# Turning the gated rows for token mixing: TensorE transposes replaced by VectorE block transposes and a DRAM round trip

## The chip, the cores and the metric

The kernel runs on one core of one Trainium2 chip. The metric is the device time of one execution in microseconds; the time before is the median of three runs. All times below are microseconds unless they are marked ns.

## What is computed

Attention with sigmoid weights over 4 batches of 12 heads (448 rows, head size 64), then a gated feed-forward block on x of 4 x 448 x 768, then a token and channel mixer:

```python
xk = mu_k * x + (1 - mu_k) * x_prev        # x_prev: x one row earlier
xr = mu_r * x + (1 - mu_r) * x_prev
k  = np.maximum(xk @ w_k, 0.0)             # 768 -> 1024
v  = k * k @ w_v                           # 1024 -> 768
y  = sigmoid(xr @ w_r) * v                 # the gated rows
h  = np.maximum(y.transpose(0, 2, 1) @ w_tok1, 0.0) @ w_tok2   # 448 -> 256 -> 448
u  = y + h.transpose(0, 2, 1)
out = u + np.maximum(u @ w_ch1, 0.0) @ w_ch2                   # 768 -> 1536 -> 768
```

The kernel keeps channels on partitions and tokens in the free dimension. Only the token mixing contracts over tokens, so y has to be turned once before it.

## The kernel before, in words

The four batches are worked on in two halves of two batches (`for b0 in range(0, B, 2)`, L526): `attention`, `first_part`, `second_part`. Each of the 768 channels is in one of NT = 6 tiles of 128; a tile holds 896 tokens of two batches (W = 2 S). Every product of this kernel is made of three float32r passes: operands are split into a high and a low part, and high times high, high times low and low times high are summed (`products`, L336). `products` runs a first column piece of 512 and one of 384 over all inner tiles, and after each second inner tile it calls `tick()`, which emits one pending step of the weight pipeline.

The weight pipeline (L264 to L310) is in program order on each engine. A weight w is loaded by SP into one of two `raw` buffers (`w_raw`), formed by two ScalarE instructions (`w_form`, L236 and L237), joined by two VectorE instructions (`w_join`, L240 and L243; the end of a join frees the raw buffer and lets SP issue the load of the weight after next), its high part is written by ScalarE (`w_high`, L281) and its low part by VectorE (`w_low`, L285). Weights of `w_v` and `w_tok1` are 128x512, all others here are 128x768.

`first_part` first makes r (L421), then k (L430), then six rows of `w_v` products (L441). "Row m" below is the m-th of these six: TensorE multiplies with two weights (part 0 and part 1), and at its end VectorE multiplies the result into `rows[:, m]` (L448). These are the gated rows. In row m, in the second column piece of part 0, `y_transpose(m - 1)` (L362) turns the row before: eight TensorE transposes against an identity (L368) into a PSUM tile, then ScalarE and VectorE write the high and the low part (L370, L371), and for the last 64 tokens a high part on partitions 0 to 63 and a low part on 64 to 127 (L372, L373). The last row, `y_transpose(5)`, is turned inside the first piece of the first token product.

The token mixing is six small products of w_tok1 and six of w_tok2. In this text tok1(p) is the p-th piece of L455 (p = 0 to 2, each makes h1 of two channel tiles m = 2p and 2p + 1; ScalarE L467, VectorE L468 write its two parts), and tok2(m) the product of L474 that adds h of tile m to `rows[:, m]` (L480). Before, all three tok1 come first and then all six tok2. `u`, the input of the channel mixing, is split into two parts by ScalarE (L481) and VectorE (L472), after each tok2. `u`, `y` and the inputs of k lie in the same memory `two`, so that `u` can't be written before the last use of `y`. The first product of `second_part` ("f = 0" below) runs its two column pieces in turn, tile by tile, so that it needs u of tile 5 last.

The order of instructions of each engine is the order of the program (`manual_schedule`, L67): no scheduler moves them, and an engine that waits holds all that is behind it.

Of the kernel before, what the change touches and what calls it, by code (L numbers as in the profile page):

```python
# [8 lines left out]

F32 = mybir.dt.float32  # L10
F32R = mybir.dt.float32r
# [11 lines left out]
P = 128  # L23
# [3 lines left out]
W = 2 * S  # L27

WIDE = ((0, 512), (512, W - 512))
WARM = 26  # L30
HALF = 3 * P + S

# [6 lines left out]
def kernel(  # L39
# [23 lines left out]
    wraw, wpool, wsplit = pool("wraw", 2), pool("wpool", 2), pool("wsplit", 3)  # L63
    tmps = pool("tmps", 2)
    psum = pool("psum", 4, space=PSUM)

    ctx.enter_context(tc.manual_schedule())  # L67

# [4 lines left out]


    warm = const.tile([P, 1], F32, tag="warm", name="warm")
    ident = const.tile([P, P], F32, tag="ident", name="ident")
    mus = {n: [const.tile([P, NT], F32, tag=m + n, name=m + n) for m in ("mu", "om")] for n in "kr"}
    xes = [const.tile([P, 2, 1 + S], F32, tag="xe%d" % i, name="xe") for i in range(NT)]
    const.tile([P, 8], F32, tag="pad", name="pad")
# [33 lines left out]
    def new_ps():  # L113
        return psum.tile([P, 1024], F32, tag="ps", name="ps")
# [29 lines left out]
    load_v(0)  # L144
    load_v(1)

    make_identity(nc, ident)

    for t in xes:
        POOL.memset(t[:, :, 0:1], 0.0)  # L150

    att = {}

# [205 lines left out]
    def against(w, x, kt):  # L359
        return [(w[0][:, t], w[1][:, t], x[0][:, t], x[1][:, t]) for t in range(kt)]  # L360

    def y_transpose(m):  # L362
        ps = new_ps()
        psv = ps.rearrange("p (r b c) -> p r b c", r=4, b=2)
        for r in range(4):
            n = P if r < 3 else TAIL
            for b in range(2):
                PE.transpose(psv[:n, r, b], rows[:, m, b * S + r * P : b * S + r * P + n], ident)  # L368
        hi, lo = (t[:, :, m] for t in y)
        ACT.copy(hi[:, :3], psv[:, :3])  # L370
        DVE.tensor_tensor(out=lo[:, :3], in0=psv[:, :3], in1=f32(hi[:, :3]), op=ALU.subtract)  # L371
        ACT.copy(hi[:TAIL, 3], psv[:TAIL, 3])  # L372
        DVE.tensor_tensor(out=hi[TAIL:, 3], in0=psv[:TAIL, 3], in1=f32(hi[:TAIL, 3]), op=ALU.subtract)  # L373

    def attention(b0):
        end = (b0 + 2) * NPAIR

        def load_more(i):
            if i + 3 < end:
                load_kq(i + 3)  # L380
                load_v(i + 2)
                load_v(i + 3)
            if i + 4 < end:
                load_kq(i + 4)

        for t in range(NT):
            i, xe = b0 * NPAIR + 2 * t, xes[t]
            if t == 0:
                load_kq(i + 2)
            else:  # L390
                load_more(i)
            scores(i)
            if i == 0:
                score_tails(i)
            scores(i + 1)
            if t == 0:
                if i:
                    score_tails(i)
                load_more(i)
                if i == 0:  # L400
                    w_raw(2)
            if t + 1 < NT:
                split_kq(i + 2)
                split_kq(i + 3)
            if b0 == 0 and 1 <= t < 5:
                w_form(t)
                w_join(t)
                w_raw(t + 2)
                w_high(min(t - 1, 3))
                w_low(min(t - 1, 3))  # L410
            ps = [values(i), values(i + 1)]
            if t + 1 < NT:
                score_tails(i + 2)
            value_tails(i, ps[0], xe)
            value_tails(i + 1, ps[1], xe)
            mix("r", t, xr, xe)

    def first_part(b0):
        if b0 == 0:
            tok2_load()  # L420
        for m in range(NT):  # L421
            w = weights()
            ps = new_ps()
            products(ps, WIDE, against(w, xr, NT), in_turn=m == 0)
            ACT.activation(rows[:, m], ps[:, :W], AF.Sigmoid)
            mix("k", m, xk, xes[m])
            if b0 == 0 and m < 3:
                tok2_stage(m)

        for m in range(F // P):  # L430
            w = weights()
            ps = new_ps()
            products(ps, WIDE, against(w, xk, NT))
            hi, lo = kk(m)
            t = tmps.tile([P, W], F32, tag="tmp", name="sq")
            ACT.activation(t, ps[:, :W], AF.Relu)
            DVE.tensor_tensor(out=t, in0=t, in1=t, op=ALU.mult)
            ACT.copy(hi, t)
            DVE.tensor_tensor(out=lo, in0=t, in1=f32(hi), op=ALU.subtract)

        for m in range(NT):  # L441
            ps = new_ps()
            for part in range(2):
                w = weights()
                parts = [(w[0][:, t], w[1][:, t], *kk(4 * part + t)) for t in range(4)]
                hooks = {0: lambda: y_transpose(m - 1)} if m and part == 0 else {}
                products(ps, WIDE, parts, 4 * part, 8, hooks)
            DVE.tensor_tensor(out=rows[:, m], in0=rows[:, m], in1=ps[:, :W], op=ALU.mult)  # L448

        wt1 = [weights()]  # L450
        i = use[0]
        use[0] += 1
        wt1.append(halves.pop(i))
        due.extend([lambda: w_form(i + 4), lambda: None, lambda: w_join(i + 4), lambda: w_raw(i + 6)])
        for piece in range(3):  # L455
            ps = new_ps()
            ms = slice(2 * piece, 2 * piece + 2)
            for j in range(2):
                wh, wl = wt1[j]
                x = [t[:, :, ms].rearrange("p r m b c -> p r (m b c)") for t in y]  # L460
                parts = [(wh[:, r], wl[:, r], x[0][:, r], x[1][:, r] if r < 3 else None) for r in range(4)]
                products(ps[:, j * 512 : (j + 1) * 512], ((0, 512),), parts)
                if piece == 0 and j == 1:
                    y_transpose(NT - 1)
# [4 lines left out]
        due.extend([lambda: w_high(i + 3), lambda: w_low(i + 3)])  # L469
# [4 lines left out]
        for m in range(NT):  # L474
# [6 lines left out]
            ACT.copy(u[0][:, m], rows[:, m])  # L481
            if m:
                u_low(m - 1)
        u_low(NT - 1)

    def second_part(b0):
        for half in range(2):
# [44 lines left out]
def lay_out(x):  # L532

    import numpy as np

    def chunks(w, parts=1):

        kt = w.shape[0] // (P * parts)
        w = w.reshape(parts, kt, P, w.shape[1] // P, P).transpose(3, 0, 2, 1, 4)
        return w.reshape(-1, P, kt * P)  # L540

    qt = x["q"].transpose(0, 1, 3, 2).reshape(B * NPAIR, P, S)
    kt = x["k"].transpose(0, 1, 3, 2).reshape(B * NPAIR, P, S)
# [4 lines left out]
    y = {  # L548
        "q": qt,
        "k": np.concatenate([kt[:, :, 3 * P :], kt[:, :, : 3 * P]], axis=2),  # L550
        "v": np.concatenate([head, tail], axis=2),
        "moe_mu_k": x["moe_mu_k"].reshape(NT, P).T,
        "moe_mu_r": x["moe_mu_r"].reshape(NT, P).T,
        "moe_w_k": chunks(x["moe_w_k"]),
        "moe_w_v": chunks(x["moe_w_v"], 2),
        "moe_w_r": chunks(x["moe_w_r"]),
        "moe2_w_tok1": chunks(np.concatenate([x["moe2_w_tok1"], x["moe2_w_tok1"][3 * P :]])),
        "moe2_w_tok2": x["moe2_w_tok2"],
        "moe2_w_ch1": chunks(x["moe2_w_ch1"]),
        "moe2_w_ch2": chunks(x["moe2_w_ch2"], 2),  # L560
    }
# [44 lines left out]
```

## Time and profile before

| | |
|---|---|
| time, median of 3 runs | 869.82 us (869.79 to 870.35) |
| the profiled execution's own time | 870.03 us |
| its span | 868.2 us |
| PE busy | 863.7 us (99%) |
| PEld (weight loads, beside PE) | 728.8 us (84%) |
| DVE busy | 539.3 us (62%) |
| ACT busy | 407.1 us (47%) |
| POOL busy | 1.0 us |
| moved by DMA | 98.12 MB |

PE is TensorE, DVE is VectorE, ACT is ScalarE, POOL is GpSimd and SP the engine that issues most DMAs. The profiled execution took 0.21 us more than the median. The busy share says how much of the span an engine had an instruction; where a time of the engine is not on the chain that ends last, it costs nothing.

### The profile page before, as it was taken

To read this page: it belongs to the slowest core of one execution; us is meant where nothing else is said; L and a number is where in the kernel's file an instruction comes from. 1 tells how busy PE (TensorE), PEld (TensorE's weight loads), DVE (VectorE), ACT (ScalarE), POOL (GpSimd) and SP (SyncE) were. 2 spreads that over 40 slices of the span, in tenths; PEclk is the share of its full clock that TensorE was granted. 3 is DMA by queue.
4 is the path that set the end of the run, shared out by engine and by line. 5 is a ranking of instruction groups with operands and counts; after the bars stand their busy time and mean duration, and the time that the engine had idled before them with its cause. 6 is when DMAs were issued, how large, how long until landed. Compare 5 with 4: busy or idle time off the path is not lost.

```text
span 868.2 us, 11307 instructions
## 1 busy us (share of the span) xinstructions
PE 863.7 (99%) x4616; PEld 728.8 (84%) x4616; DVE 539.3 (62%) x610; ACT 407.1 (47%) x538; POOL 1.0 (0%) x13
## 2 busy tenths in 40 slices
PE   9999999999999999999999999999999999999998
PEld 5558989899888989898955598989998998989897
DVE  4877966556676555555656598666566755554551
ACT  6884455444544433443356644455445444334420
POOL 0000000000000000000000000000000000000000
PEclk9999999999999999999999999999999999999999
DMA  8532332233412333334664133222334033333321
GB/s 279 194 129 79 109 109 85 74 98 97 140 67 75 110 123 102 103 108 164 223 206 132 40 109 109 88 94 74 97 98 165 18 109 109 109 109 110 109 100 63
DMA packets 29571, 98.12 MB, mean 113 GB/s; under 512 B 3536, under 2 KB 15952, under 8 KB 29520
## 3 DMA queue, kind: packets, MB, share of 16 engines
q1 hardware_dynamic: 29232, 96.95, 33.6%
q8 instruction: 36, 0.59, 0.3%
q10 hardware_dynamic: 288, 0.46, 0.1%
q14 instruction: 15, 0.12, 0.1%
HBM read 91.89 MB, written 5.51 MB: 112 GB/s over the span
## 4 chain that ended last, share of the span: by engine, by line
PE 99%; DVE 0%; issue 0%; POOL 0%; POOLq 0%
PE ps L347 84%; PE ps L209 6%; PE ps L182 6%; PE ps L198 1%; PE ps L368 1%; PE ps L217 1%; PE ps L141 0%; DVE rows L506 0%; POOL rows L138 0%; POOLq L592 0%
## 5 line engine op out<-in xcount | busy, mean ns | idle before, releaser
L347 PE MATMUL ps<-one,whi 128*128 128x512 f32 (+1 forms) x1152 | 323.6, 363 | 0.0
L347 PE MATMUL ps<-two,whi 128*128 128x512 f32 (+1 forms) x1044 | 295.8, 365 | 0.0
L347 PEld LDWEIGHTS ps<-one,whi 128*128 128x128 f32 x1152 | 211.5, 188 | 24.8 <-issue 1.4
L347 PEld LDWEIGHTS ps<-two,whi 128*128 128x128 f32 x1044 | 192.5, 188 | 23.1 <-DVE two L371 0.4
L347 PE MATMUL ps<-one,wlo 128*128 128x512 f32 (+1 forms) x576 | 207.3, 363 | 0.0
L347 PE MATMUL ps<-two,wlo 128*128 128x512 f32 (+1 forms) x528 | 191.1, 366 | 0.0
L281 ACT CAST whi<-wd 128x768 fp32r<-128x768 f32 (+1 forms) x104 | 80.7, 776 | 134.6 <-PE ps L347 93.6
L347 PEld LDWEIGHTS ps<-one,wlo 128*128 128x128 f32 x576 | 107.9, 188 | 11.3
L240 DVE SCALAR_TENSOR_TENSOR wd<-wd,raw 128x768 uint32<-128x768 uint32 (+1 forms) x104 | 92.2, 886 | 32.8 <-ACT raw L237 32.5
L347 PEld LDWEIGHTS ps<-two,wlo 128*128 128x128 f32 x528 | 99.0, 188 | 11.4
L285 DVE TENSOR_TENSOR wlo<-wd,whi 128x768 fp32r<-128x768 f32 (+1 forms) x104 | 91.6, 880 | 9.4 <-ACT whi L281 8.9
L243 DVE SCALAR_TENSOR_TENSOR wd<-raw,wd 128x768 uint32<-128x768 uint32 (+1 forms) x104 | 92.2, 886 | 3.6
L236 ACT ACTIVATE wd<-raw 128x768 f32<-128x768 f32 (+1 forms) x104 | 88.4, 850 | 3.9 <-DMA raw<-in_moe_w_ch_dram 2.3
L237 ACT ACTIVATE raw<-raw 128x768 uint32<-128x768 uint32 (+1 forms) x104 | 86.9, 836 | 0.0
L494 DVE SCALAR_TENSOR_TENSOR one<-ps,one 128x896 fp32r<-128x896 f32 x24 | 26.2, 1092 | 71.0 <-ACT one L493 71.0
L512 DVE TENSOR_TENSOR rows<-rows,ps 128x896 f32<-128x896 f32 x23 | 25.0, 1087 | 67.8 <-PE ps L347 67.8
L493 ACT ACTIVATE one<-ps 128x896 fp32r<-128x896 f32 x24 | 22.1, 921 | 95.8 <-PE ps L347 95.8
L190 ACT ACTIVATE rows<-ps 128x896 f32<-128x896 f32 x72 | 60.2, 967 | 9.4 <-PE ps L182 8.9
L209 PE MATMUL ps<-rows,vn 128*64 128x448 f32 x288 | 56.8, 543 | 0.0
L182 PEld LDWEIGHTS ps<-two 64*128 64x128 f32 x414 | 37.9, 184 | 10.9 <-PE ps L198 6.3
L209 PEld LDWEIGHTS ps<-rows,vn 128*64 128x64 f32 x288 | 19.6, 137 | 31.9 <-issue 27.6
L182 PE MATMUL ps<-two 64*128 64x448 f32 x414 | 45.2, 368 | 0.0
(67 smaller groups left out, 533.8 us busy)
## 6 DMA issues: line engine op xcount, KB each, us to landing
raw<-in_moe_w_ch_dram SPq DMA_DIRECT2D x48, 768.0 KB, 4.1
raw<-in_moe_w_k_dram SPq DMA_DIRECT2D x16, 768.0 KB, 4.2
raw<-in_moe_w_v_dram SPq DMA_DIRECT2D x24, 512.0 KB, 3.6
raw<-in_moe_w_r_dram SPq DMA_DIRECT2D x12, 768.0 KB, 4.3
vn<-in_v_dram SPq DMA_DIRECT2D x24, 224.0 KB, 4.3
kq<-in_k_dram SPq DMA_DIRECT2D x23, 224.0 KB, 4.2
kq<-in_q_dram SPq DMA_DIRECT2D x23, 224.0 KB, 4.3
out_dram<-rows SPq DMA_DIRECT2D x23, 224.0 KB, 2.1
```

The source lines that it names most:

```text
L182: PE.matmul(ps[:, h * 512 : h * 512 + S], x[me, c * P : (c + 1) * P], y[me], start=(n == 0), stop=(n == len(passes) - 1),)
L190: ACT.activation(a, banks(ps), AF.Sigmoid, bias=-math.log(S), scale=1.0 / math.sqrt(D))
L209: PE.matmul(ps[h * D : h * D + D, :S], vns[i % 4][:, 3 * h + c], att[i % 2, c][:, h], start=(c == 0), stop=False)
L236: ACT.activation(f32(dst), f32(raw[..., 1]), AF.Copy, scale=2.0**-112)
L237: ACT.activation(raw[..., 0], raw[..., 0], AF.Copy, bias=0.4375, scale=0.875 * 2.0**-29)
L240: DVE.scalar_tensor_tensor(out=dst, in0=dst, scalar=3, in1=raw[..., 0], op0=ALU.logical_shift_left, op1=ALU.bitwise_or)
L243: DVE.scalar_tensor_tensor(out=dst, in0=raw[..., 1], scalar=0x80000000, in1=dst, op0=ALU.bitwise_and, op1=ALU.bitwise_or)
L281: ACT.copy(halves[i][0], forms[i])
L285: DVE.tensor_tensor(out=halves[i][1], in0=forms.pop(i), in1=f32(halves[i][0]), op=ALU.subtract)
L347: PE.matmul(ps[:, a : a + cols], w, x[:, a : a + cols], start=(i == 0 and n == 0), stop=(i == count - 1 and n == len(passes) - 1),)
L494: DVE.scalar_tensor_tensor(out=lo, in0=ps[:, :W], scalar=0.0, in1=f32(hi), op0=ALU.max, op1=ALU.subtract)
L512: DVE.tensor_tensor(out=rows[:, m], in0=rows[:, m], in1=ps[:, :W], op=ALU.add)
```

## The change

The TensorE transposes, their PSUM tile and the identity are gone. In their place, for each row m:

- `y_turn(m)`: three VectorE STREAM_TRANSPOSE instructions turn 32x32 blocks of `rows[:, m]` into a buffer `turned` (768 columns of both batches, then the last 64 tokens twice with 128 columns each).
- `y_out(m)`: a DMA that ScalarE issues writes the buffer (512 KB) to a DRAM tile `blocks`.
- `y_in(m)`: a DMA that ScalarE issues reads it back into `staged` in another order, so that the blocks of one token group stand beside each other: 4 pieces of 1 KB for each of 128 partitions. It waits for `y_out(m)`.
- `y_split(m)`: ScalarE writes the high part (L405) and VectorE the low part (L406). For the last 64 tokens, which stand on the partitions twice, ScalarE multiplies with `sign` (L407), VectorE multiplies the staged copy with `latter` (L409) and adds (L410), so that half of the partitions get the high part and half the low part.

`turned` and `staged` (two buffers each) lie in the memory of `xes`, whose first column is therefore zeroed by POOL again in each `attention`. The rows of w_tok1 are permuted on the host to the order that the blocks have. `latter` and `sign` are made once, by POOL and VectorE, at the start.

The token mixing is written in another order: tok1(0), tok1(1), tok2(0), tok2(1), tok2(2), tok1(2), tok2(3), tok2(4), tok2(5), with the split of row 4 behind tok1(0), the split of row 5 behind tok2(1), and all splits of u behind tok1(2).

```diff
-    def y_transpose(m):
...
+    def y_turn(m):
+        src = beside(rows[:, m])
+        dst = turned[m % 2].rearrange("p d r b c -> p b r d c")
+        DVE.transpose(dst[:, :, :3], src[:, :, : 3 * P].rearrange("p b (r d c) -> p b r d c", r=3, d=4))
+        for d in (0, 2):
+            DVE.transpose(dst[:, :, 3, d : d + 2], src[:, :, 3 * P :].rearrange("p b (d c) -> p b d c", d=2))
+
+    blocks = []
+
+    def y_out(m):
+        blocks.append(dram.tile([P, 8 * P], F32, tag="blocks", name="blocks"))
+        ACT.dma_start(out=blocks[0], in_=turned[m % 2].rearrange("p d r b c -> p (d r b c)"))
+
+    def y_in(m):
+        ACT.dma_start(
+            out=staged[m % 2].rearrange("p s r b c -> p s (r b c)"),
+            in_=blocks.pop().rearrange("(s p) (d n) -> (p d) s n", s=4, d=4),
+        )
+
+    def y_split(m):
+        src = staged[m % 2].rearrange("p s r b c -> p r b s c")
+        hi, lo = (t[:, :, m].rearrange("p r b (s c) -> p r b s c", c=BLK) for t in y)
+        ACT.copy(hi[:, :3], src[:, :3])
+        DVE.tensor_tensor(out=lo[:, :3], in0=src[:, :3], in1=f32(hi[:, :3]), op=ALU.subtract)
+        ACT.activation(hi[:, 3], src[:, 3], AF.Identity, scale=sign)
+        ends = staged[m % 2][:, :, 3].rearrange("p s b c -> p s (b c)")
+        DVE.tensor_scalar(out=ends, in0=ends, scalar1=latter, scalar2=None, op0=ALU.mult)
+        DVE.tensor_tensor(out=hi[:, 3], in0=f32(hi[:, 3]), in1=src[:, 3], op=ALU.add)
...
-                hooks = {0: lambda: y_transpose(m - 1)} if m and part == 0 else {}
+                hooks = {}
+                if m and part == 0:
+                    hooks = {0: lambda: y_turn(m - 1), 3: lambda: y_out(m - 1)}
+                    if m > 1:
+                        hooks[2] = lambda: y_split(m - 2)
+                elif m:
+                    hooks = {7: lambda: y_in(m - 1)}
                 products(ps, WIDE, parts, 4 * part, 8, hooks)
             DVE.tensor_tensor(out=rows[:, m], in0=rows[:, m], in1=ps[:, :W], op=ALU.mult)
 
+        y_turn(NT - 1)
         wt1 = [weights()]
...
+        tok1(0, {0: lambda: y_out(NT - 1)})
+        y_split(NT - 2)
+        tok1(1, {0: lambda: y_in(NT - 1)})
+        tok2(0)
+        tok2(1)
+        y_split(NT - 1)
+        tok2(2)
+        tok1(2)
+        due.extend([lambda: w_high(i + 3), lambda: w_low(i + 3)])
+        for m in range(3, NT):
+            u_high(m - 3)
+            u_low(m - 3)
+            tok2(m)
+        for m in range(3, NT):
+            u_high(m)
+            u_low(m)
```

The first place where the order matters is ScalarE in a row of w_v products. Before, from the turned row of one w_v row to that of the next:

```order
L370 CAST two<-ps 128x3x256
L372 CAST two<-ps 64x256
L281 CAST whi<-wd 128x512
L236 ACTIVATE wd<-raw 128x512
L237 ACTIVATE raw<-raw 128x512
L281 CAST whi<-wd 128x512
L236 ACTIVATE wd<-raw 128x512
L237 ACTIVATE raw<-raw 128x512
```

And in the changed kernel, from one `y_in` (L397) to the next `y_out` (L394); `blocks` is the DRAM tile, and `xe` the memory of `turned` and `staged`:

```order
L397 DMA xe<-blocks 128x4x256
L300 CAST whi<-wd 128x512
L255 ACTIVATE wd<-raw 128x512
L256 ACTIVATE raw<-raw 128x512
L405 CAST two<-xe 128x3x256
L407 ACTIVATE two<-xe,sign 128x256
L394 DMA blocks<-xe 128x1024
```

Two DMA issues with their waits stand between the steps of two weights, and the casts that read PSUM now read what the DMA brought back.

The second place is VectorE from the last gated row to the first second-layer token product. Before (L448 is the product of row 5, L468 the low part of h1, three pieces in a row):

```order
L448 TENSOR_TENSOR rows<-rows,ps 128x896
L285 TENSOR_TENSOR wlo<-wd,whi 128x768
L240 SCALAR_TENSOR_TENSOR wd<-wd,raw 128x768
L243 SCALAR_TENSOR_TENSOR wd<-raw,wd 128x768
L240 SCALAR_TENSOR_TENSOR wd<-wd,raw 128x768
L243 SCALAR_TENSOR_TENSOR wd<-raw,wd 128x768
L371 TENSOR_TENSOR two<-ps,two 128x3x256
L373 TENSOR_TENSOR two<-ps,two 64x256
L468 SCALAR_TENSOR_TENSOR one<-ps,one 128x2x512 x3
```

The same stretch in the changed kernel, from the last of the block transposes of row 5 to the second piece of h1 (L515 is the low part of h1):

```order
L388 STREAM_TRANSPOSE xe<-rows 128x2x2x32 x2
L304 TENSOR_TENSOR wlo<-wd,whi 128x768
L259 SCALAR_TENSOR_TENSOR wd<-wd,raw 128x768
L262 SCALAR_TENSOR_TENSOR wd<-raw,wd 128x768
L259 SCALAR_TENSOR_TENSOR wd<-wd,raw 128x768
L262 SCALAR_TENSOR_TENSOR wd<-raw,wd 128x768
L515 SCALAR_TENSOR_TENSOR one<-ps,one 128x2x512
L406 TENSOR_TENSOR two<-xe,two 128x3x256
L409 TENSOR_SCALAR xe<-xe,latter 128x4x64
L410 TENSOR_TENSOR two<-two,xe 128x256
L515 SCALAR_TENSOR_TENSOR one<-ps,one 128x2x512
```

The two joins of weights (L259, L262) still stand ahead of the low part of h1 of the first piece, and the split of row 4 now stands between the first and the second piece.

The third place is VectorE at the end of the token mixing. Before, the last two additions of h (L480), the low parts of u (L472) and the low part of a weight:

```order
L480 TENSOR_TENSOR rows<-rows,ps 128x896
L472 TENSOR_TENSOR two<-rows,two 128x896
L480 TENSOR_TENSOR rows<-rows,ps 128x896
L472 TENSOR_TENSOR two<-rows,two 128x896 x2
L285 TENSOR_TENSOR wlo<-wd,whi 128x768
```

In the changed kernel, from the third piece of h1 to the last low part of u (L518 is the low part of u, L529 adds h to the rows):

```order
L515 SCALAR_TENSOR_TENSOR one<-ps,one 128x2x512
L518 TENSOR_TENSOR two<-rows,two 128x896
L304 TENSOR_TENSOR wlo<-wd,whi 128x768
L529 TENSOR_TENSOR rows<-rows,ps 128x896
L518 TENSOR_TENSOR two<-rows,two 128x896
L529 TENSOR_TENSOR rows<-rows,ps 128x896
L518 TENSOR_TENSOR two<-rows,two 128x896
L529 TENSOR_TENSOR rows<-rows,ps 128x896
L518 TENSOR_TENSOR two<-rows,two 128x896 x3
```

Three low parts of u now follow the last addition, where before it was two.

## Rows read from the trace of the kernel before

**Rows 1.** The page: busy time, and the granted clock in 40 slices.
```profile
PE 863.7 (99%) x4616; PEld 728.8 (84%) x4616; DVE 539.3 (62%) x610; ACT 407.1 (47%) x538; POOL 1.0 (0%) x13
PEclk9999999999999999999999999999999999999999
```

**Rows 2.** Chain that ended last, in order of time: start, us, what.
```profile
181.23 0.87 PE ps L368 x8
182.10 9.65 PE ps L347 x48
...
665.27 0.87 PE ps L368 x8
```

**Rows 3.** Timeline of PE, token mixing, first half: start, us, instruction.
```profile
230.43 0.61 PE L347 MATMUL ps<-two,whi 128*128 128x512 f32 x2
...
246.36 0.36 PE L347 MATMUL ps<-wt2h,one 128*128 128x448 f32 x1
```

**Rows 4.** Groups by line and form: busy us, mean ns, idle before.
```profile
L285 DVE TENSOR_TENSOR wlo<-wd,whi 128x768 fp32r<-128x768 f32 x76 | 72.3, 951 | 0.5
L281 ACT CAST whi<-wd 128x768 fp32r<-128x768 f32 x76 | 63.4, 834 | 95.9 <-PE ps L347 91.8 <-DVE wd L243 4.1
L243 DVE SCALAR_TENSOR_TENSOR wd<-raw,wd 128x512 uint32<-128x512 uint32 x28 | 19.4, 692 | 1.0
L285 DVE TENSOR_TENSOR wlo<-wd,whi 128x512 fp32r<-128x512 f32 x28 | 19.3, 688 | 8.9 <-ACT whi L281 8.9
L237 ACT ACTIVATE raw<-raw 128x512 uint32<-128x512 uint32 x28 | 18.4, 657 | 0.0
L281 ACT CAST whi<-wd 128x512 fp32r<-128x512 f32 x28 | 17.4, 620 | 38.6 <-DVE wd L243 36.8 <-PE ps L347 1.8
L156 DVE CAST two<-kq 128x832 fp32r<-128x832 f32 x23 | 13.5, 588 | 14.2 <-DMA kq<-in_q_dram 14.2
L227 DVE TENSOR_SCALAR mix<-xe,omk 128x896 f32<-128x896 f32 x12 | 8.2, 680 | 0.0
L373 DVE TENSOR_TENSOR two<-ps,two 64x256 fp32r<-64x256 f32 x12 | 5.0, 418 | 5.2 <-ACT two L372 5.2
```

**Rows 5.** Timeline of DVE, the last gated row and the first h1, first half.
```profile
231.64 0.96 DVE L243 SCALAR_TENSOR_TENSOR wd<-raw,wd 128x768 uint32<-128x768 uint32 x1
232.52 1.08 DVE L448 TENSOR_TENSOR rows<-rows,ps 128x896 f32<-128x896 f32 x1
...
238.60 0.96 DVE L240 SCALAR_TENSOR_TENSOR wd<-wd,raw 128x768 uint32<-128x768 uint32 x1 [1.50 <-ACT raw L237]
239.60 0.96 DVE L243 SCALAR_TENSOR_TENSOR wd<-raw,wd 128x768 uint32<-128x768 uint32 x1
...
242.78 2.36 DVE L468 SCALAR_TENSOR_TENSOR one<-ps,one 128x1024 fp32r<-128x1024 f32 x2 [0.51 <-ACT one L467]
```

**Rows 6.** Timeline of ACT, the same stretch.
```profile
236.87 0.90 ACT L236 ACTIVATE wd<-raw 128x768 f32<-128x768 f32 x1 [1.75 <-DMA raw<-in_moe_w_ch_dram]
237.66 0.91 ACT L237 ACTIVATE raw<-raw 128x768 uint32<-128x768 uint32 x1
...
241.72 1.93 ACT L467 ACTIVATE one<-ps 128x1024 fp32r<-128x1024 f32 x2
```

**Rows 7.** DMA issues of the whole span: count, KB each, median us to landing.
```profile
raw<-in_moe_w_v_dram SPq DMA_DIRECT2D x24, 512.0 KB, 3.6
vn<-in_v_dram SPq DMA_DIRECT2D x24, 224.0 KB, 4.3
...
out_dram<-rows SPq DMA_DIRECT2D x23, 224.0 KB, 2.1
```

**Rows 8.** DMA issues of 0 to 30 us.
```profile
raw<-in_moe_w_r_dram SPq DMA_DIRECT2D x3, 768.0 KB, 6.6
```

**Rows 9.** Timeline of DVE, end of the token mixing, first half.
```profile
261.15 1.09 DVE L480 TENSOR_TENSOR rows<-rows,ps 128x896 f32<-128x896 f32 x1 [0.34 <-PE ps L347]
262.15 2.19 DVE L472 TENSOR_TENSOR two<-rows,two 128x896 fp32r<-128x896 f32 x2
```

More of the change, by code (lines that the diff above doesn't have):

```diff
@@ L7 @@
 from concourse._compat import with_exitstack
-from concourse.masks import make_identity
 F32 = mybir.dt.float32
@@ L29 @@
 WIDE = ((0, 512), (512, W - 512))
+BLK = 32
 WARM = 26
@@ L65 @@
     psum = pool("psum", 4, space=PSUM)
+    dram = pool("dram", 2, space=bass.MemoryType.DRAM)
     ctx.enter_context(tc.manual_schedule())
     warm = const.tile([P, 1], F32, tag="warm", name="warm")
-    ident = const.tile([P, P], F32, tag="ident", name="ident")
+    latter, sign = (const.tile([P, 1], F32, tag=n, name=n) for n in ("latter", "sign"))
     mus = {n: [const.tile([P, NT], F32, tag=m + n, name=m + n) for m in ("mu", "om")] for n in "kr"}
-    xes = [const.tile([P, 2, 1 + S], F32, tag="xe%d" % i, name="xe") for i in range(NT)]
-    const.tile([P, 8], F32, tag="pad", name="pad")
+    xes = const.tile([P, NT * 2 * (1 + S)], F32, tag="xe", name="xe")
+    const.tile([P, 152], F32, tag="pad", name="pad")
+    turned, staged = (
+        [xes[:, (i + n) * 8 * P : (i + n + 1) * 8 * P].rearrange("p (d r b c) -> p d r b c", d=4, r=4, b=2) for n in range(2)]
+        for i in (0, 2)
+    )
+    xes = [
+        xes[:, t * 2 * (1 + S) : (t + 1) * 2 * (1 + S)].rearrange("p (b n) -> p b n", b=2) for t in range(NT)
+    ]
     one = const.tile([P, 2 * NT * W], F32R, tag="one", name="one")
@@ L145 @@
     load_v(1)
-    make_identity(nc, ident)
-    for t in xes:
-        POOL.memset(t[:, :, 0:1], 0.0)
+    marks = rows[:, NT - 2, : 2 * BLK]
+    POOL.memset(marks, 0.0)
+    POOL.affine_select(
+        out=marks,
+        in_=marks,
+        compare_op=ALU.not_equal,
+        fill=1.0,
+        base=-2,
+        pattern=[[-4, BLK], [-1, 2]],
+        channel_multiplier=1,
+    )
+    DVE.tensor_reduce(out=latter, in_=marks, axis=mybir.AxisListType.X, op=ALU.add)
+    DVE.tensor_scalar(out=sign, in0=latter, scalar1=-2.0, scalar2=1.0, op0=ALU.mult, op1=ALU.add)
     att = {}
@@ L360, in against @@
         return [(w[0][:, t], w[1][:, t], x[0][:, t], x[1][:, t]) for t in range(kt)]
-    def y_transpose(m):
[L363 to L373, printed above, removed]
+    def y_turn(m):
[12 more added lines that the diff above has]
+            in_=blocks.pop().rearrange("(s p) (d n) -> (p d) s n", s=4, d=4),
+        )
+    def y_split(m):
[7 more added lines that the diff above has]
+        DVE.tensor_tensor(out=hi[:, 3], in0=f32(hi[:, 3]), in1=src[:, 3], op=ALU.add)
     def attention(b0):
+        for xe in xes:
+            POOL.memset(xe[:, :, 0:1], 0.0)
         end = (b0 + 2) * NPAIR
@@ L454, in first_part, with tok1 @@
         due.extend([lambda: w_form(i + 4), lambda: None, lambda: w_join(i + 4), lambda: w_raw(i + 6)])
-        for piece in range(3):
+        def tok1(piece, hooks={}):
             ps = new_ps()
@@ L462, in first_part @@
                 products(ps[:, j * 512 : (j + 1) * 512], ((0, 512),), parts)
-                if piece == 0 and j == 1:
-                    y_transpose(NT - 1)
+                if j in hooks:
+                    hooks[j]()
             hi, lo = (t[:, :, ms].rearrange("p j m b c -> p j (m b c)") for t in h1)
@@ L468, in first_part, with u_high, tok2 @@
             DVE.scalar_tensor_tensor(out=lo, in0=psv, scalar=0.0, in1=f32(hi), op0=ALU.max, op1=ALU.subtract)
-        due.extend([lambda: w_high(i + 3), lambda: w_low(i + 3)])
         def u_low(m):
             DVE.tensor_tensor(out=u[1][:, m], in0=rows[:, m], in1=f32(u[0][:, m]), op=ALU.subtract)
-        for m in range(NT):
+        def u_high(m):
+            ACT.copy(u[0][:, m], rows[:, m])
+        def tok2(m):
             ps = new_ps()
@@ L480, in first_part @@
             DVE.tensor_tensor(out=r, in0=r, in1=banks(ps), op=ALU.add)
[L481 to L484, printed above, removed]
+        tok1(0, {0: lambda: y_out(NT - 1)})
[14 more added lines that the diff above has]
+            u_low(m)
     def second_part(b0):
@@ L556, in lay_out @@
         "moe_w_r": chunks(x["moe_w_r"]),
-        "moe2_w_tok1": chunks(np.concatenate([x["moe2_w_tok1"], x["moe2_w_tok1"][3 * P :]])),
+        "moe2_w_tok1": chunks(
+            np.concatenate([x["moe2_w_tok1"], x["moe2_w_tok1"][3 * P :]])
+            .reshape(4, 4, BLK, TOK)
+            .transpose(0, 2, 1, 3)
+            .reshape(4 * P, TOK)
+        ),
         "moe2_w_tok2": x["moe2_w_tok2"],
```

## The prediction

> **What bounds the kernel now.** I read the page first: TensorE is busy 99% of the span and its granted clock is at full speed in all 40 slices (2.4 GHz, the upper of its two levels), while VectorE is at 62% and ScalarE at 47% [rows 1]. Then the chain that ended last: it runs on TensorE from start to end, so whatever TensorE no longer does comes off the time, unless it waits instead. In that chain the eight transposes of one gated row stand as pieces of 0.87 us, the first at 181.23 and the last, of twelve, at 665.27; between two of them lie 9.65 us of products, 48 matmuls of 0.20 us on average [rows 2]. So one row of w_v products is 9.65 us of TensorE, and everything that the change does to y on other engines has this period to hide in. Last I read the timelines of the three engines around the token mixing, because the change reorders it [rows 3, 5, 6].
>
> **What goes.** Twelve groups of 0.87 us are 10.44 us of TensorE, all on the path [rows 2]. The PSUM reads of ScalarE and VectorE that followed them go too; they were beside other work.
>
> **What comes, off TensorE.** Twelve times: the block transposes, a 512 KB write to DRAM, a 512 KB read back, and a split.
>
> *Block transposes on VectorE.* No row shows one. Below: a VectorE copy of 832 columns takes 0.59 [rows 4], so 768 and twice 128 take no less than 0.9. Above: twice the 0.95 of a two-operand instruction on 768 columns and twice 0.42 for each short one [rows 4], 2.8. I take 1.3, one column per step like the two-operand instruction but without its second operand, nearer to the lower end. The Trainium skill ("VectorE: DVE Perf Modes", Rules for kernel authors) speaks against the change: transpose 128x128 on TensorE where PSUM will do, VectorE turning 32x32 blocks alone. By that rule the transposes would stay and the time with them, at 870; the rows show that TensorE is the engine without room.
>
> *Write.* 224 KB of output land in 2.1 us, 512 KB of w_v in 3.6 [rows 7]; I take 2.7, and up to 3.6 it changes nothing, since ScalarE has two weight steps to do before it needs the write.
>
> *Read back.* No row shows 1 KB packets out of fresh DRAM data. Below: 3.6 us, the 512 KB loads of w_v in rows of 4 KB. Above: 6.6 us, loads of 768 KB in the crowded first 30 us [rows 8]. I take 4.3, the v loads: they are the nearest in packet size (1.8 KB) and also run beside others [rows 7].
>
> *Split.* High part 0.83 on ScalarE, low part 0.95 on VectorE [rows 4]; the tail's mask and sum on 256 columns 0.3 each, between a tensor-scalar at 0.68 for 896 columns and the old tail at 0.42 [rows 4].
>
> **The chain in a row of w_v products.** ScalarE and VectorE work in program order, so these steps chain with the weight pipeline. Times after the row's start on TensorE: the product of the row before is written by 1.3 (0.2 for TensorE's last column, 1.08 [rows 5]), the low part of a weight by 2.0 (0.69 [rows 4]), the transposes by 3.3, the split by 4.9 (0.95 + 0.6 + hand-over), the join of a weight by 6.3 (two of 0.69), ScalarE's high part by 7.0 (0.62), the next weight's forming by 8.3 (two of 0.66 [rows 4]), and then `y_in` is issued. The next split waits for it. From one `y_in` to the next: 4.3 landing, 0.83 high part, 0.95 + 0.6 VectorE's split, 1.4 join, 0.7 high part with hand-over, 1.3 forming, 0.1 for hand-overs: 10.2 us, against a row of 9.65. So from row 2 on the chain slips 0.55 per row: 8.3, 8.85, 9.4, and in row 5 9.95 plus 0.4, since the weight formed there has 768 columns. TensorE doesn't feel that in the rows: each weight's low part is ready over 5 us before its use.
>
> **What it does to the token mixing.** Let T be the start of tok1(0), 230.43 in the first half [rows 3]. The join behind that forming takes 1.95 and ends at 10.35 + 2.0 - 9.65 = T + 2.7; before, it ended at 232.60, T + 2.2 [rows 5]. From there on the order of both kernels is the same up to h1: this join frees a raw buffer, the load lands 4.27 later (236.87), forming takes 1.70 (to 238.57), the join 1.99 (to 240.56) [rows 5, 6], and only then VectorE comes to the low part of h1 of tok1(0), 1.2 us [rows 5]. With 0.1 for hand-overs and 0.2 because `y_in` of row 4 shares the DMA engines with that load, it ends at T + 12.2. The block transposes of row 5, 1.3 us, fall into VectorE's wait for the load (1.50 idle even at its end [rows 5]) and cost nothing.
>
> tok2(0) needs that low part at its third matmul. Before, it came behind all three tok1, at 246.36, T + 15.9, and the low part was there at 243.9. Without the transposes, (15.93 - 0.87) / 3 = 5.02 us is one tok1; now tok2(0) stands behind two, and its third matmul is due at T + 10.04 + 0.4 = T + 10.4. **TensorE waits 1.8 us, in each half.** This is the price of moving tok2 ahead: 5 us of cover are gone where 2.4 were spare.
>
> **Edits that I cost at nothing, with their cover.** `y_in` of row 5 is issued at about T + 11 and lands by T + 16; tok1(2) starts behind three tok2 of 12 x 0.20 us, T + 19, and VectorE's own queue sets its split, so 1 to 2 us are spare. tok2(4) needs h1 of tok1(2), one tok2 later (2.8 with two matmuls): 1.0 on ScalarE [rows 6] and 1.2 on VectorE are ready at 2.4, spare 0.4. The u splits now begin behind tok1(2): VectorE has 1.2 + 0.95 + three additions and six low parts of about 1.05 (261.15 to 262.15 to the next [rows 9]), 11.6 us from 1.3 on, ready at 12.9; f = 0 reaches the low part of tile 5 at 7.2 + 5 x 1.2 + 0.4 = 13.6. Spare 0.7. If that cover fails, the excess is lost twice. The masks at the start, POOL's twelve memsets and the host's order of w_tok1 stand ahead of or beside idle engines.
>
> **The sum.** 870.03, the profiled execution's time, minus 10.44, plus 2 x 1.8 = 863.2. That execution is 0.21 over the median of the runs shown, so against the median I say **862.9**.
>
> **The rivals.**
>
> *The chain doesn't slip.* With the read back at 3.6 us, as w_v's loads [rows 7], the chain is 9.5, under the row; the join ends at T + 1.0, the low part at T + 10.4, and the waits are 0 to 0.4 per half: 859.6 to 860.4, say 860.0. For it: fewer bytes are in flight than in the v loads. Against: 512 packets instead of 128. The Trainium skill ("DMA: Bandwidth & Descriptors", Anatomy of one DMA) gives 2.0 us plus bytes at 436 GB/s, 3.2 us for 512 KB as an estimate, by which this rival would hold; w_v's loads show 3.6 [rows 7].
>
> *The round trip through DRAM becomes the bound (slower).* Place: ScalarE at the high part of a staged row (L405), with the weight steps behind it. Each 0.1 us of the read back above 3.75 slips three rows, 0.3 us per half. The wait eats the whole 5.2 us per half at 1.8 + 3 x (t - 4.3) = 5.2, t = 5.4 us; at 6.0, between the v loads and the crowded 6.6 [rows 8], it is 6.9 per half, plus about 1 for the second weight of tok1, which then comes late as well: 870.03 - 10.44 + 2 x 7.9 = 875.4. For it: the read shares the engines with two weight loads per row. Against: the mean load is far from the crowded one.
>
> *VectorE becomes the bound of the rows.* With transposes at 2.8 us, product 1.08, low part 0.69, split 1.6, join 1.4, ScalarE's 0.7 and 1.3, and the second join 1.4 chain to 11.0 us; four rows slip 1.3 each and the wait is about 6.3 per half: 872.2. It decides from 1.5 us of transposes on.
>
> *TensorE's gain is not a gain.* Nothing speaks for it: the 0.87 stands alone in the chain.
>
> **How the numbers follow.** Forecast (waits of 0.9 to 3.5 per half, 861.2 to 866.4) 0.50; no slip 0.32; slower by the round trip 0.08; VectorE 0.05; between forecast and no change 0.05. The lower end, 859.5, is all of the 10.44; the upper, 867.5, is the read back at 5.0, with 1 in 10 above. A measurement of this kernel tells about 0.2%, 1.7 us: faster 0.87, same 0.04, slower 0.09.
>
> **What would show it.** PE's and PEld's counts fall by 96 each [rows 1]; in the chain, rows follow each other by 9.65. Right: one wait of TensorE per half, at the third matmul of tok2(0), on VectorE's low part of h1, 1 to 3 us, and `y_in` landing in 4 to 4.6. Wrong: no wait there (first rival), weight loads of tok1 waiting on VectorE (the slower ones), a wait at tok1(2) for y, or one at f = 0 for u.

## The result and the profile after

The changed kernel takes 860.12 us in the median of four runs (859.85 to 860.19), the kernel before beside it 869.81: a ratio of 0.9888, 95% interval 0.9871 to 0.9905. The forecast was 862.9, the first rival's time 860.0. The profiled execution took 860.19 with a span of 858.4, 9.8 less than before. What the page says of it, to be held against [rows 1]:

```profile
PE 853.6 (99%) x4520; PEld 718.6 (84%) x4520; DVE 557.9 (65%) x660; ACT 407.7 (47%) x538; POOL 1.7 (0%) x19
PEclk9999999999999999999999999999999999999999
```

96 instructions are gone from PE and from PEld, and the granted clock is full throughout. In the chain that ended last (start, us, what) the products of a half, which before were cut into pieces by the 0.87 us of transposes [rows 2], are now one piece:

```profile
67.32 363.14 PE ps L366 x1794
...
491.69 363.17 PE ps L366 x1794
```

Before, the same stretch ran from 66.74 to 434.92, 368.18 us; less six times 0.87, 362.96. So the first half costs 0.18 more than its bare products, and the second, by the same sum, 0.13. The span's 9.8 are then 10.44 less 0.31 for the two halves and 0.58 for a later start, plus 0.28 that the second attention took less. The start is not the change's doing: in the repeat of the changed kernel the products begin at 66.90, and in the run below that has the start of the kernel before and only the new order at 67.11.

One wait on the new work is left in the rows of PEld (engine, line, what it waited for: us in total, times, longest). It is at the place forecast, on the low part of h1, in the first of the two halves:

```profile
PEld ps L366 <- DVE one L515: 0.3, 1, 0.3
```

It should have been 1.8 us in each. What the new operations take, in the groups by form (busy us, mean ns, idle before):

```profile
L386 DVE STREAM_TRANSPOSE xe<-rows 128x768 f32<-128x768 f32 x12 | 11.7, 971 | 0.1
L406 DVE TENSOR_TENSOR two<-xe,two 128x768 fp32r<-128x768 f32 x12 | 11.2, 932 | 0.1
L388 DVE STREAM_TRANSPOSE xe<-rows 128x128 f32<-128x128 f32 x24 | 6.1, 291 | 0.4
L410 DVE TENSOR_TENSOR two<-two,xe 128x256 fp32r<-128x256 f32 x12 | 5.1, 426 | 0.4
L409 DVE TENSOR_SCALAR xe<-xe,latter 128x256 f32<-128x256 f32 x12 | 4.2, 354 | 1.3
```

The block transposes of a row are 0.97 + 2 x 0.29 = 1.55 us (forecast 1.3), the tail of the split 0.78 (forecast 0.6). And the DMA issues (KB each, median us to landing), beside [rows 7]:

```profile
raw<-in_moe_w_v_dram SPq DMA_DIRECT2D x24, 512.0 KB, 3.6
blocks<-xe ACTq DMA_DIRECT2D x12, 512.0 KB, 2.7
xe<-blocks ACTq DMA_DIRECT2D x12, 512.0 KB, 5.2
```

The write is as forecast. The read back takes 5.2, where I said 4.3. So all three unknowns came out dearer than I took them or equal, and yet the wait that they were to cause is not there. The reason stands in ScalarE's timeline (ACTq are DMAs that it issues), in the row that starts on TensorE at 188.08:

```profile
194.57 0.62 ACT L300 CAST whi<-wd 128x512 fp32r<-128x512 f32 x1 [3.62 <-DVE wd L262]
194.77 0.38 ACTq L397 DMA_DIRECT2D xe<-blocks  x1
195.10 0.68 ACT L255 ACTIVATE wd<-raw 128x512 f32<-128x512 f32 x1
195.67 0.67 ACT L256 ACTIVATE raw<-raw 128x512 uint32<-128x512 uint32 x1
...
199.63 0.84 ACT L405 CAST two<-xe 128x768 fp32r<-128x768 f32 x1
```

In the program `y_in` (L397) stands behind L300, L255 and L256. It is issued 0.20 us after L300 *starts*, ahead of both forming instructions. That it does stand behind them shows in the row before, where the read had to wait for its write (issued at 181.82, landed 2.7 later, at 184.5); there both had started when it went out:

```profile
183.79 0.67 ACT L255 ACTIVATE wd<-raw 128x512 f32<-128x512 f32 x1
184.36 0.65 ACT L256 ACTIVATE raw<-raw 128x512 uint32<-128x512 uint32 x1
184.58 0.38 ACTq L397 DMA_DIRECT2D xe<-blocks  x1
```

What does hold the read in the later rows is, by these times, L300's own wait for VectorE (3.62 above): in rows 2 to 5 of this half the writes have landed 0.7 to 0.9 us before the reads go out, and each read goes out 0.14 to 0.20 after L300 starts. The five rows' reads go out 6.2, 6.7, 6.6, 6.9 and 6.6 us after the start of their row: nothing slips. The next row on VectorE shows what bounds it instead:

```profile
197.95 1.09 DVE L493 TENSOR_TENSOR rows<-rows,ps 128x896 f32<-128x896 f32 x1 [0.15 <-PE ps L366]
198.95 0.68 DVE L304 TENSOR_TENSOR wlo<-wd,whi 128x512 fp32r<-128x512 f32 x1
199.55 0.97 DVE L386 STREAM_TRANSPOSE xe<-rows 128x768 f32<-128x768 f32 x1
200.56 0.51 DVE L388 STREAM_TRANSPOSE xe<-rows 128x128 f32<-128x128 f32 x2
200.99 0.92 DVE L406 TENSOR_TENSOR two<-xe,two 128x768 fp32r<-128x768 f32 x1
...
204.90 0.69 DVE L304 TENSOR_TENSOR wlo<-wd,whi 128x512 fp32r<-128x512 f32 x1 [0.74 <-ACT whi L300]
206.04 0.69 DVE L259 SCALAR_TENSOR_TENSOR wd<-wd,raw 128x512 uint32<-128x512 uint32 x1 [0.45 <-ACT raw L256]
...
207.61 1.09 DVE L493 TENSOR_TENSOR rows<-rows,ps 128x896 f32<-128x896 f32 x1 [0.15 <-PE ps L366]
```

The low part L406 follows the transposes at once; the read, landed by 199.6, is not what it waits for. It is only just off the chain: in the next row the read takes 5.6, lands at 210.0, and L406 starts 0.2 later in its row. VectorE's own chain, with two short waits for ScalarE in it, fills 9.51 of the row's 9.66 us; the 0.15 idle before the product is all that is spare. VectorE's tail of the first half, where T is now 226.75:

```profile
226.81 0.96 DVE L262 SCALAR_TENSOR_TENSOR wd<-raw,wd 128x768 uint32<-128x768 uint32 x1
...
235.04 0.96 DVE L262 SCALAR_TENSOR_TENSOR wd<-raw,wd 128x768 uint32<-128x768 uint32 x1
235.92 1.22 DVE L515 SCALAR_TENSOR_TENSOR one<-ps,one 128x1024 fp32r<-128x1024 f32 x1
```

The join ends at T + 1.0 (forecast T + 2.7) and the low part of h1 at 237.14, T + 10.4 (forecast T + 12.2), the moment at which tok2(0) wants it.

### The profile page after: what moved, and what is told of

The parts are those of the page before. It is cut to its first block, busy times and chain, and to the rows that moved or that the text cites. A ratio compares the mean times of both kernels' runs of the same rounds, so it can differ in the third digit from the quotient of the medians.

```text
span 858.4 us, 11255 instructions
## 1 busy us (share of the span) xinstructions
PE 853.6 (99%) x4520; PEld 718.6 (84%) x4520; DVE 557.9 (65%) x660; ACT 407.7 (47%) x538; POOL 1.7 (0%) x19
## 4 chain that ended last, share of the span: by engine, by line
PE 99%; DMA 1%; DVE 0%; SPq 0%; issue 0%; DVEq 0%
PE ps L366 85%; PE ps L228 7%; PE ps L201 5%; PE ps L217 1%; PE ps L236 1%; DMA kq<-in_q_dram 1%; DVE two L176 0%; DVE two L175 0%; DVE rows L569 0%; SPq L132 0%; SPq L141 0%; SPq L140 0%; DVEq L175 0%
## 5 line engine op out<-in xcount | busy, mean ns | idle before, releaser
L300 ACT CAST whi<-wd 128x768 fp32r<-128x768 f32 (+1 forms) x104 | 80.8, 777 | 149.3 <-PE ps L366 103.9
L259 DVE SCALAR_TENSOR_TENSOR wd<-wd,raw 128x768 uint32<-128x768 uint32 (+1 forms) x104 | 92.0, 885 | 29.4 <-ACT raw L256 29.4
L262 DVE SCALAR_TENSOR_TENSOR wd<-raw,wd 128x768 uint32<-128x768 uint32 (+1 forms) x104 | 92.2, 886 | 3.6
L255 ACT ACTIVATE wd<-raw 128x768 f32<-128x768 f32 (+1 forms) x104 | 88.3, 849 | 4.5 <-DMA raw<-in_moe_w_ch_dram 2.0
L256 ACT ACTIVATE raw<-raw 128x768 uint32<-128x768 uint32 (+1 forms) x104 | 87.2, 838 | 0.0
```

Source lines behind the costliest of these rows:

```text
L255: ACT.activation(f32(dst), f32(raw[..., 1]), AF.Copy, scale=2.0**-112)
L256: ACT.activation(raw[..., 0], raw[..., 0], AF.Copy, bias=0.4375, scale=0.875 * 2.0**-29)
L259: DVE.scalar_tensor_tensor(out=dst, in0=dst, scalar=3, in1=raw[..., 0], op0=ALU.logical_shift_left, op1=ALU.bitwise_or)
L262: DVE.scalar_tensor_tensor(out=dst, in0=raw[..., 1], scalar=0x80000000, in1=dst, op0=ALU.bitwise_and, op1=ALU.bitwise_or)
L300: ACT.copy(halves[i][0], forms[i])
```

## The experiments

All ratios are to the kernel before, run beside each. My theory after the result: the early issue of `y_in` takes the read off the chain; VectorE's row is the next bound, with 0.15 us to spare; each part of the change alone gains nothing or loses. The rival: the place of the issue doesn't matter, and the chain has room.

**The changed kernel again.** No edit.

> The changed kernel once more, unaltered, as the base for the runs beside it, and to see whether the 0.58 us by which its first attention ended later than before (products begin at 67.32 instead of 66.74) belongs to the change. Theory: it belongs to the landing of the first loads and varies from run to run; the products begin between 66.5 and 67.5 and the time is 859.5 to 860.5. Rival: the masks that POOL and VectorE now make at the start cost it; the products begin at 67.3 again.

860.14 (859.15 to 860.35), ratio 0.9886 [0.9871, 0.9901]. The span is 858.5, the products begin at 66.90 and take 362.97 and 363.01 in the two halves, and the wait on L515 is not there at all. The median read lands in 5.0 here.

**The read held back to its place in the program.**

```diff
+    def bind(m):
+        ACT.copy(staged[m % 2][:, 0, 0, 0, 0:1], warm)
...
-                    hooks = {7: lambda: y_in(m - 1)}
+                    hooks = {7: lambda: (bind(m - 1), y_in(m - 1))}
```

> In the rows a copy of one column by ScalarE into the read's destination stands between the forming of the weight and y_in, so that the read can't be issued before the forming is done, as the prediction assumed it to be. Theory (the prediction's chain was right but for the place of the issue; in the trace the read is issued 1.6 us before the forming ends): with 5.2 us of landing the chain from one read to the next is 11.4 us against a row of 9.66, rows 3 to 5 slip 1.75 each, the join moves to about T + 6.2, the second weight of tok1 is 0.5 late and tok2(0) waits some 5.5 us per half: 870.5 to 872.5. Rival (the read has room enough wherever it is issued): 860 to 861.

869.49 (864.54 to 871.38), ratio 0.9989 [0.9974, 1.0004]: by the median nothing is left of the gain. The ten executions differ more than those of the other kernels, from 864.54 at a mean granted clock of 1.000 to 871.38 at 0.996. ScalarE's timeline, what PE waited for, and three pieces of the chain that ended last (start, us, what; line numbers are 3 higher here behind L400):

```profile
193.78 0.62 ACT L300 CAST whi<-wd 128x512 fp32r<-128x512 f32 x1 [3.64 <-DVE wd L262]
195.69 0.38 ACTq L397 DMA_DIRECT2D xe<-blocks  x1
```

```profile
PE ps L366 <- DVE one L518: 3.1, 2, 1.5
PE ps L366 <- ACT one L517: 3.0, 2, 1.7
```

```profile
624.84 3.98 DMA xe<-blocks
...
634.87 4.57 DMA xe<-blocks
...
645.47 4.84 DMA xe<-blocks
```

The read goes out 1.91 us after L300 starts instead of 0.20, and from one read to the next it is now 11.32, 10.50, 10.44 and 10.69 us, against a row of 9.66: the chain of the prediction, slipping, and the reads of these rows are on the chain that ended last. The copy itself takes under 0.2 us of ScalarE in a row, so without it the cycle would, as an estimate, still be over 10.2. TensorE then waits some 3 us in each half at tok2(0), where the theory had 5.5, since the read itself, issued later, took 4.3 here and not 5.2. 6.1 of the 9.3 us of span are these waits. The rest goes with the granted clock, 0.996 on the mean: it stands at 0.50 (1.2 GHz) from 240 to 243 and from 670 to 673, after the waits, about 1.5 us of lost work each time. The time came out 1 us below the theory's range; the rival, 860 to 861, falls.

**The transposes twice.**

```diff
-                    hooks = {0: lambda: y_turn(m - 1), 3: lambda: y_out(m - 1)}
+                    hooks = {0: lambda: (y_turn(m - 1), y_turn(m - 1)), 3: lambda: y_out(m - 1)}
...
         y_turn(NT - 1)
+        y_turn(NT - 1)
```

> Each y_turn is written twice, 1.45 us more of VectorE per row. Theory (VectorE's chain of product, low part, transposes, split, join, high part, forming, join fills 9.5 of the 9.66 us of a row, so it has 0.15 us to spare): rows 2 to 5 slip 1.3 us each, the join that frees the raw buffer moves from T + 1.0 to about T + 6.3, the low part of h1 to T + 15.7, and TensorE waits some 5.4 us per half at tok2(0), perhaps 0.6 at the second weight of tok1: 870.5 to 872. Rival (VectorE is busy 65% of the span and takes it in its idle time): 860 to 861.

875.63 (875.42 to 875.86), ratio 1.0066 [1.0051, 1.0081]. VectorE has no room for 1.55 us more in a row, as the theory says, and the rival falls; the size was forecast 4 us too small. In the chain of the first half (start, us, what) the product of a row now follows that of the row before by 10.97 and 10.95 us, 1.3 more than TensorE's row, and all that lies between is VectorE's work and the steps of ScalarE that it waits for, the read's issue (0.38) among them:

```profile
198.74 0.78 DVE rows L493
...
209.71 0.78 DVE rows L493
...
220.66 0.78 DVE rows L493
```

The waits of TensorE are those of VectorE's late rows, ScalarE's L515 (the high part of h1) among them:

```profile
PE ps L366 <- ACT one L515: 6.2, 2, 3.1
PE ps L366 <- DVE one L516: 2.7, 2, 1.5
```

With 0.6 on the high part of a weight that is 9.5 of the 15.2 us of span. The rest goes with the granted clock: in the first half it was 0.50 in all of 240 to 246, behind an idle TensorE (no work at all from 238 to 240).

**One part of the change at a time.** First the new transposes with the token mixing in its old order:

```diff
-        tok2(0)
-        tok2(1)
         y_split(NT - 1)
-        tok2(2)
         tok1(2)
         due.extend([lambda: w_high(i + 3), lambda: w_low(i + 3)])
-        for m in range(3, NT):
-            u_high(m - 3)
-            u_low(m - 3)
+        for m in range(NT):
             tok2(m)
-        for m in range(3, NT):
             u_high(m)
-            u_low(m)
+            if m:
+                u_low(m - 1)
+        u_low(NT - 1)
```

> The block transposes and the DRAM round trip stay, the token mixing is put back into the order of before: tok1(0), tok1(1), tok1(2), then six tok2, each followed by its split of u. Theory (the new order is there to hide the round trip of row 5): tok1(2) is due at T + 10 and the low part of row 5 is there at T + 14.3, so TensorE waits 4 us per half: 868. Rival (the round trip is short enough to hide behind tok1(0) and tok1(1)): 860.

871.56 (870.09 to 872.92), ratio 1.0016 [1.0007, 1.0025]: no gain, a trace of a loss. TensorE waits at tok1(2) for row 5. Its timeline, and the windows of the same stretch (us, PE, PEld, DVE, ACT, POOL busy with counts, granted clock, DMA share, GB/s):

```profile
239.24 0.50 PE L366 MATMUL ps<-two,whi 128*128 128x512 f32 x1 [2.87 <-ACT two L405]
240.25 0.50 PE L366 MATMUL ps<-two,whi 128*128 128x512 f32 x1 [0.51 <-DVE two L406]
```

```profile
236.00:239.00 3.00, 0.37 (x2) 0.00 (x0) 2.86 (x5) 1.67 (x2) 0.10 (x1) 1.00 1.06 402
...
241.00:242.00 1.00, 1.00 (x4) 0.73 (x4) 0.12 (x1) 0.00 (x0) 0.13 (x2) 0.73 0.02 8
242.00:243.00 1.00, 1.00 (x4) 0.79 (x3) 0.00 (x0) 0.00 (x0) 0.00 (x0) 0.50 0.00 0
...
245.00:246.00 1.00, 1.00 (x6) 0.83 (x5) 0.00 (x0) 0.00 (x0) 0.00 (x0) 1.00 0.08 16
```

The two waits are 3.4 us in this half and 6.7 in both, less than the 8 expected, yet the time is 3.6 above the 868 expected. Behind them the clock falls to 0.50 and the matmuls stand 0.43 apart, where at full clock it is 0.23. So the wait is paid once as idle time and then, in part, again as slow work: the span is 11.1 longer than that of the changed kernel, and 6.7 of it are the waits.

Then the new order with the TensorE transposes of before (its token mixing is that of the change, without `y_out`, `y_in` and the two `y_split`):

> The kernel of before with its TensorE transposes, but with the new order of the token mixing. Theory: no TensorE work goes; tok2(0) now needs the low part of h1 of the first piece at T + 11.3, but before it came at T + 13.5, behind the two copies of the last turned row, so TensorE waits 2.2 us per half: 874. Rival (the order gains or costs nothing by itself): 869.8.

876.32 (874.92 to 877.77), ratio 1.0071 [1.0055, 1.0087]. TensorE waits at tok2(0) for h1; the rows of its waits, here with L468 and L469 as the high and the low part:

```profile
PE ps L347 <- ACT one L468: 2.6, 2, 1.3
PE ps L347 <- DVE one L469: 1.2, 2, 0.6
```

That is 1.9 per half, where I had expected 2.2. The time is 2.3 above the 874 expected, and that goes with the granted clock: the profiled execution, with a mean clock of 1.000, took 874.92, the other three 875.43 at 0.998 and 877.21 and 877.77 at 0.996. By the ratios, the new transposes alone cost 1.4 us and the order alone 6.2; together they bring 9.7. The order gives row 5 the time of three tok2 to land in. And with TensorE's transposes the PSUM reads of row 5 stand in ScalarE's and VectorE's queues ahead of h1, which the new order wants early: in the chain of this run (start, us, what) they are the two pieces ahead of it.

```profile
240.93 0.88 DVE two L371
241.83 0.36 ACT two L372
242.20 0.93 ACT one L468
243.15 1.23 DVE one L469
```

**No round trip at all.** The transposes write into `staged`, and `y_out` and `y_in` are not called.

```diff
-        dst = turned[m % 2].rearrange("p d r b c -> p b r d c")
+        dst = staged[m % 2].rearrange("p d r b c -> p b r d c")
```

> Leaves out the round trip through DRAM: the block transposes write straight into the buffer that the split reads, so that the blocks stand in the wrong order. Theory: the trip is hidden altogether, and what is left is TensorE's products alone. 859.4 to 860.4, ratio 0.988 to 0.989, no wait of TensorE at the low part of h1. Rival: the trip still costs something, through the DMA engines that it shares with the weights: 858.0 to 859.0.

859.64 (858.83 to 859.71), ratio 0.9879 [0.9864, 0.9894], with no wait at L515. The products of a half take 362.97 and 363.01 in the chain. With the trip they took 363.14 and 363.17 in the first profiled execution, and in the repeat 362.97 and 363.01, the same as without it. So 12 MB of traffic through DRAM cost between nothing and 0.3 us.

**Why the read takes 5 us.** First its pieces: 128 of 4 KB instead of 512 of 1 KB.

```diff
-            out=staged[m % 2].rearrange("p s r b c -> p s (r b c)"),
-            in_=blocks.pop().rearrange("(s p) (d n) -> (p d) s n", s=4, d=4),
+            out=staged[m % 2].rearrange("p s r b c -> p (s r b c)"),
+            in_=blocks.pop(),
```

> y_in reads the DRAM tile straight, one 4 KB piece for each partition instead of four of 1 KB, so the gated rows arrive in the wrong order for token mixing; all instructions and bytes are the same. Theory (the read back is off the path, because ScalarE issues it before the forming ahead of it is done): the landing falls from 5.2 to 3.6 to 4.3 us and the time stays, within 0.5 us of the changed kernel. Rival (the chain of the prediction, 0.3 us per half for each 0.1 us of the read): it would fall by several us if 5.2 us were being paid; it can fall by no more than the 0.3 us that TensorE waits, so a larger fall would show a loss that the waits don't show.

860.99 (859.93 to 861.54), ratio 0.9896 [0.9882, 0.9911]. The median landing is 5.0, as in the repeat of the changed kernel: the size of the pieces is not the cause, and the fall that I expected is not there. The time is 0.85 above the changed kernel beside it, more than the 0.5 expected but not clear of the noise; no fall by several us, so the rival falls. In one row of this run a weight load of w_tok1 and the read issued 0.16 us after it took 5.7 each. ScalarE waited 1.86 for the weight, and the split's high part behind its forming started 1.1 after the read had landed; TensorE then waits 1.1 us on the low part of h1 (in all 1.4). So it is the weight load that came late here, and it shows how near the edge the chain is.

Then what runs beside it:

```diff
+            n = 2 if kt == 4 else kt
+            raws[i] = raws[i][:, :n]
-            SP.dma_start(out=raws[i].rearrange("p t n e -> p (t n e)"), in_=seq[i][0])
+            SP.dma_start(out=raws[i].rearrange("p t n e -> p (t n e)"), in_=seq[i][0][:, : n * 2 * P])
```

> Leaves out half of each load of w_v and of w_tok1 (256 KB in place of 512, the missing half is formed from the other), all else as in the changed kernel. Theory: the read back takes 5 us because it shares the DMA engines with a weight load that is issued beside it. Its median landing falls to 4.0 to 4.5, the write stays at 2.6 to 2.7. Rival: the 5 us are the read's own (it follows a write of the same data, from DRAM): it stays at 4.9 or above. By both the time is that of the changed kernel, 859.5 to 860.5, since TensorE has no wait there.

859.95 (859.2 to 860.36), ratio 0.9882 [0.9865, 0.9898]. Its DMA issues:

```profile
raw<-in_moe_w_v_dram SPq DMA_DIRECT2D x24, 256.0 KB, 2.6
blocks<-xe ACTq DMA_DIRECT2D x12, 512.0 KB, 2.7
xe<-blocks ACTq DMA_DIRECT2D x12, 512.0 KB, 4.1
```

The read falls from 5.2 (5.0 in the repeat) to 4.1 with half the weight bytes, while the write, which falls between two loads, stays at 2.7. So about 1 us of the read comes from half of the weight loads' bytes, the first of which leave 0.2 us ahead of it. What the other 1.4 over the write are stays open: the other half of those bytes, or the read's own. TensorE has one wait of 0.5 on the low part of h1 in this run, where I had expected none; the time is within the range all the same.

**A weight of the tail later.** The forming, join and load that stand behind tok1(0) were put behind the split of row 4, so that the low part of h1 comes before that join:

```diff
-        due.extend([lambda: w_form(i + 4), lambda: None, lambda: w_join(i + 4), lambda: w_raw(i + 6)])
...
         y_split(NT - 2)
+        due.extend([lambda: w_form(i + 4), lambda: None, lambda: w_join(i + 4), lambda: w_raw(i + 6)])
```

> One weight's forming and join (768 columns) are moved from tok1(0) to tok1(1), so they stand behind the low part of h1 of the first piece. Theory: that low part was late (T + 10.4) only because the join of this weight stands ahead of it and its load lands at T + 5.6; now it ends near T + 7.5, TensorE's wait of 0.3 us at the third matmul of tok2(0) is gone, and the time falls by 0.3 to 0.6 us, to about 859.6. Rival: the weights of the channel mixing now come late, or the split of row 5 does; slower by 1 us or more.

859.71 (859.6 to 860.51), ratio 0.9886 [0.9869, 0.9902]. The low part of h1 ends at T + 7.5, as expected, and no wait is left. The difference to the changed kernel, 0.4 us, has the sign expected but is less than can be told apart; the repeat of the changed kernel had no wait to save either. Neither this edit nor leaving out the trip (859.64) finds more than can be measured.

## Why the prediction was right, and where it was not

- **What goes, 10.44 us: right.** The pieces of 0.87 are out of the chain and the products of a half stand in one piece. The direction and the lower end of the range rested on this term.
- **The wait, 1.8 us per half: the place was right, the size was wrong.** It was 0.3 in one half and 0 in the other, and none in the repeat. That is the difference between 862.9 and 860.1, but for the start. By the prediction's own signs (no wait there) this is the outcome of the first rival, which had 0.32, and not that of the forecast, 861.2 to 866.4, which had 0.50.
- **The step that failed** is in "the chain in a row of w_v products": "the next weight's forming by 8.3 (two of 0.66), and then `y_in` is issued". I let a DMA of ScalarE wait until the activations ahead of it are done. It is issued while the first of three still runs; only that first one's wait for VectorE holds it. By the same sum the cycle is 10.2, less 0.5 of the high part and 1.3 of the forming, plus 0.9 for the longer read and 0.2 for the tail: 9.5, under the row's 9.66, and nothing slips. The experiment that binds the read to its place turns the cycle into 10.4 to 11.3 and takes the gain away, so this step is worth some 9 us by the medians (4 to 11 by the single executions), not 3.6.
- **That the time lies inside the range is in part luck.** The place of the issue made the forecast too slow; the read, the transposes and the split's tail, each dearer than I took them, and the slow clock behind a wait, which the sum doesn't have, made it too fast. With the read issued where the prediction has it, and landing in the 4.3 that it has, the kernel takes 869.49: above the upper end, 867.5.
- **The read back, 4.3: measured 5.2**, close to the 5.4 from which the slower rival was to decide. It didn't decide since the read is issued earlier than that rival too assumes. The Trainium skill ("DMA: Bandwidth & Descriptors", Anatomy of one DMA) gives a fit by which 512 KB would take 3.2 us as an estimate. That section gives it for DMAs that GpSimd issues, which the prediction doesn't say; those here are ScalarE's. The write (2.7) came in below it and the read, beside another load, well above.
- **The transposes, 1.3: measured 1.55**, just past the 1.5 from which the VectorE rival was to decide. With 1.55 its sum of 11.0 comes to 9.7, and the row took 9.51: of ScalarE's forming, 1.3 in that sum, VectorE has its second low part to do beside it and waits only 0.45. So it just failed to decide, and it named the next bound: doubled transposes cost 15.5 us.
- **The first rival** had the numbers of the tail to the tenth (join at T + 1.0, low part at T + 10.4, 860.0), but by another mechanism: it wanted a read of 3.6 us. That its numbers came true is luck.
- **The edits costed at nothing** were nothing: there is no wait at tok1(2), tok2(4) or f = 0, and POOL's memsets, which waited long for `blocks`, hold up nobody.
- **The rule of the Trainium skill** ("VectorE: DVE Perf Modes", Rules for kernel authors), to transpose 128x128 on TensorE where PSUM will do, does not hold in this kernel, whose TensorE is busy 99%: relieved of them it is 9.7 us faster, though only with the new order.

## What to carry to other kernels

Where one engine is busy all the time, work is well moved off it even by a long way round, here through DRAM, as long as each step of the detour fits into the period of the busy engine: add up that period on every engine it touches, and take the smallest rest (0.15 us here) as the margin. When a DMA is issued from an engine's own queue, ask what it waits for and which instruction ahead of it waits, not how long those ahead of it run; a chain that let it wait for their end was wrong by 1.7 us per row. Two edits can each bring no gain or a loss and together a gain, so a reordering is to be judged with the change that makes room for it.

## What the runs showed of the hardware

- A DMA of ScalarE passes activations that stand ahead of it: issued at 194.77, with L255 starting only at 195.10 and L256 at 195.67. A one-column copy into the DMA's target, ahead of it, moved the issue behind them (1.91 us after L300 starts). An activation ahead of it that itself waits does hold it: L300 waits 2.9 to 3.6 us for VectorE in rows 2 to 5, and the read goes out 0.14 to 0.20 after L300 starts.
- Halving the weight loads beside it makes a 512 KB read about 1 us shorter (5.2 and 5.0 in two runs with 512 KB loads, 4.1 with 256 KB), while pieces of 1 KB or 4 KB make no difference (5.2 and 5.0 against 5.0).
- A wait of TensorE can be followed by a stretch at 1.2 GHz: in the old order, after 2.87 and 0.51 us of waiting, the granted clock was 0.73, 0.50, 0.50 and 0.57 in the four microseconds from 241 on and 1.00 again at 245. It differs between executions of one kernel: in the new order alone, the profiled execution, with waits of 1.9 per half, had a mean clock of 1.000, the other three 0.996 to 0.998.
